# Softmax denominators as one row through HBM, with a different first and last chunk, in a conformer block

## The chip, the cores and the metric

The kernel runs on one core of one Trainium2 chip. The metric is the device time of one launch in microseconds (us). Five instruction streams matter: PE (TensorE, matrix multiply; its weight loads are listed as PEld), ACT (ScalarE, activation functions), DVE (VectorE, elementwise work and statistics), POOL (GpSimd) and SP (SyncE, which here only starts DMA transfers). SPq and ACTq are the streams of SP and ACT as issuers of DMA. The sixteen DMA engines move data between HBM and the on-chip memory; a DMA can also transpose a tile of 2-byte elements on its way.

## The reference

One conformer block on x of shape (2, 4000, 512) in bfloat16, with D = 512 and a feed-forward width F = 2048. LayerNorm has no weights.

```python
h = _layernorm(x);  x1 = x + 0.5 * (_silu(h @ w_ff1_a) @ w_ff1_b)
h = _layernorm(x1); q, k, v = h @ w_q, h @ w_k, h @ w_v
p = _softmax(einsum('btd,bsd->bts', q, k) * D ** -0.5)
x2 = x1 + einsum('bts,bsd->btd', p, v) @ w_o
a, b = split(_layernorm(x2) @ w_pw1);  h = a * _sigmoid(b)
dc = depthwise convolution of h over time with the 3 taps dw, then batch-normalized over all B*T rows
x3 = x2 + _silu(dc) @ w_pw2
h = _layernorm(x3); x4 = x3 + 0.5 * (_silu(h @ w_ff2_a) @ w_ff2_b)
return _layernorm(x4)
```

## The kernel before, in words

The 8,000 rows are cut into 16 chunks of 500 rows, each of four tiles of 125 rows (`TILE`). The running x stays on chip (`XT`), 125 partitions by 512 columns a tile. All matmuls but a few go through the helper `mm` (L458), so the profile gives them one line; the tile names tell them apart. `s` is one of four PSUM banks handed out in turn by `sbank`, `y` one of four accumulation banks.

The program runs in stages. `ff1` goes through the 16 chunks: LayerNorm, first matmul with `Wa` and Silu, second matmul with `Wb`, residual. Then `attention` goes through 16 groups of 500 queries, eight for each of the two batches. Then comes the convolution, then `ff2` through the 16 chunks, with the closing LayerNorm and the stores of the output.

The order of work is written out by hand. `lags` holds matmuls that are emitted some steps after the step that makes their operand. `after(n, fn)` has `fn` emitted n ticks later, and `tick` is called once at the end of each step. Within an engine, instructions run in the order in which they are emitted; `Sync` adds the semaphore waits that the buffers ask for. A DMA takes its semaphore from a small set used in rotation, and the queue that issues it also waits until the previous DMA on that semaphore has landed. A record (`Buf`) stands for a piece of memory; a write to it waits for the write and the reads before it.

An attention group has 32 steps kt, one for each tile of 125 keys (padded to 128). In each step PE makes the scores (four matmuls into an `s` bank), ACT their exponentials `P`, and DVE adds `P` to a running sum `acc` (L749; L746 in the first step). The matmuls of `P` with the values are emitted four steps later, into the four `y` banks. So a group's last values matmuls come in step 3 of the next group; `finish_queries` follows them. It copies the four `y` banks to `OT`, two on ACT (L483) and two on DVE (L787), and splits `acc` into a bfloat16 high part `ahi` (L791) and the rest `alo` (L792). Two ticks later `sums` turns these into the 500 denominators: for each of four tiles, two matmuls with the keys' partial sums as weights and a column of ones as the moving operand, which leaves the denominators on the query partitions of one PSUM tile, and a reciprocal on DVE (L802). From the fourth tick on, one a tick, `project` multiplies `OT` with the folded weights `Wvo` and the residual scales by the reciprocal (L591). When the last of the four is out, `done` starts the LayerNorm of the chunk (`ln_job`), whose last steps are four DMA transposes on SP (L491). Parts of the convolution (`conv_b`, `conv_a`, `taps_beside`) are emitted in steps 22 and 27 of the next group and 1 and 6 of the one after. In group 7 and the start of group 8 the keys of the second batch are loaded over those of the first (`second_keys`, one load and one DMA transpose on SP a step).

At the start (`program`) x's first chunk is loaded by two DMAs on SP, of 80 and 45 rows (`ROWS`), followed on SP by 16 weight loads with the second chunk of x among them. A Silu on one column brings ACT's table in, and 20 matmuls of zeros (`warm`) run on PE. The first chunk's normalized rows are transposed by PE (`transpose_pe`, L473) and copied out of PSUM by ACT and DVE. Further on, in the eighth step of the first chunk, `weights` has SP load w_q, w_k, w_v by DMA transposes and w_o by a plain DMA; `fold_weights` on PE needs them.

At the end `ff_last` handles the last chunk: it makes all 16 first matmuls, then all second matmuls tile by tile, so that the residual, LayerNorm and store of one tile run beside the matmuls of the next. Each tile's store is cut into 80 rows on SP and 45 on ACT (`store_out`, L665).

Of the kernel before, what the change touches and what calls it, by code (L numbers as in the profile page):

```python
# [52 lines left out]
class Sync:  # L53
# [105 lines left out]
    def dma(self, e, dkey, *fns, reads=(), writes=()):  # L159
        req = self._required(reads, writes)  # L160
        prev = self.count[dkey]
        if prev > 0:
            v = req.get(dkey)
            if v is None or v.val < prev:
                req[dkey] = Ev(dkey, prev, {})
        self._emit_waits(e, req)
        for fn in fns:
            fn(self.eng[e]).then_inc(self.sem[dkey], 16)
            self.count[dkey] += 16
        ev = Ev(dkey, self.count[dkey], dict(self.clock[e]))  # L170
        self._bind(ev, reads, writes)
        return ev
# [46 lines left out]
class Conformer:  # L219
    LN_SLOTS = 4  # L220
    NP = 8

    ROWS = ((0, 80), (80, TILE))
# [13 lines left out]
    def memory(self):  # L237
# [70 lines left out]
        self.zero, self.b_zero = self.P[0], self.b_P[0]  # L308
# [41 lines left out]

        self.late = [A.view(k * 1024, CHUNK) for k in range(FC - self.NP)]
        self.b_late = [A.buf("late", k * 1024, 1000) for k in range(FC - self.NP)]
# [44 lines left out]
        self.b_m3 = [C.buf("m3", oLT + 4096 + j * 250, 250) for j in range(TPC)]  # L397
        self.mx = small(TCB, parts=TILE)
# [9 lines left out]
        self.b_Y = [Buf("y%d" % i, excl=True) for i in range(4)]  # L408
        self.keys2 = nc.dram_tensor("keys2", [TB * 128, D], BF16, kind="Internal").ap()
# [51 lines left out]
    def warm(self, n):  # L461

        ps, b_ps = self.sbank()
        for k in range(n):
            self.mm(ps[:, 0:CHUNK], self.ident, self.zero, True, True, [self.b_ident, self.b_zero], b_ps,
                    inc=k == n - 1)

    def transpose_pe(self, ti, s, eng):

        ps, b_ps = self.sbank()  # L470
        out = ps[:, 0:DC * 64].bitcast(BF16).rearrange("p (c k) -> p c k", c=DC)
        for cc in range(DC):
            self.S.op("PE", lambda e, cc=cc: e.transpose(  # L473
                out[:, cc, 0:TILE], self.ltm[ti][0:TILE, cc * 128:(cc + 1) * 128], self.ident[0:TILE, 0:TILE]),
                reads=[self.b_ltm[ti], self.b_ident], writes=[b_ps], inc=cc == DC - 1)
        dst, src = self.lnT[s][:, ti, :, 0:TILE], out[:, :, 0:TILE]
        if eng == "ACT":
            self.act(dst, src, AF.Copy, [b_ps], [self.b_lnT[s][ti]])
        else:
            self.S.op("DVE", lambda e: e.tensor_copy(dst, src), reads=[b_ps], writes=[self.b_lnT[s][ti]])  # L480

# [3 lines left out]
    def load(self, dst, src, writes, eng="SP", reads=()):  # L485
        k = self.S.dsems[self.nxt("ld", 16)]
        return self.S.dma(eng, k, lambda e: e.dma_start(dst, src), reads=reads, writes=writes)  # L487

    def transpose(self, dst, src, reads, writes):
        k = self.S.dsems[16 + self.nxt("tr", 12)]  # L490
        return self.S.dma("SP", k, lambda e: e.dma_start_transpose(dst, src), reads=reads, writes=writes)  # L491

    def load_rows(self, dst, src, writes):
        k = self.S.dsems[self.nxt("ld", 16)]
        return self.S.dma("SP", k, *[lambda e, lo=lo, hi=hi: e.dma_start(dst[lo:hi], src[lo:hi])
                                     for lo, hi in self.ROWS], writes=writes)

# [4 lines left out]
    def load_x(self, c):  # L502
        if c == 0:
            src = self.x_flat[0:CHUNK, :].rearrange("(t p) d -> p t d", p=TILE)
            self.load_rows(self.XTc[0], src, self.bx[0:TPC])
# [90 lines left out]
    def ff_first(self, c, f, p, b_p):  # L596
        ps, b_ps = self.sbank()
        out = ps[:, 0:CHUNK].rearrange("p (t k) -> p t k", t=TPC)
        for cc in range(DC):
            self.mm(out, self.Wa[:, cc, f * 128:(f + 1) * 128], self.lnT[c % 2][:, :, cc, 0:TILE],  # L600
                    cc == 0, cc == DC - 1, [self.b_Wa[f * self.NWA // FC]] + self.b_lnT[c % 2], b_ps)
        self.act(p, ps[:, 0:CHUNK], AF.Silu, [b_ps], [b_p])

    def ff_second(self, f, ti, p, b_p, inc):
        self.mm(self.Yb[ti][0:TILE, :], p[:, ti * TILE:(ti + 1) * TILE], self.Wb[:, f, :],
                f == 0, f == FC - 1, [self.b_Wb[f], b_p], self.b_Y[ti], inc=inc)

    def ff_chunk(self, c, old, hook, done):

        pops = {0: old // 2, 1: old - old // 2, 2: 0, 3: 0, 7: 2, 11: 2}  # L610
        for f in range(FC):
            s = self.nxt("P", self.NP)
            self.ff_first(c, f, self.P[s], self.b_P[s])

            def second(f=f, s=s):
                for ti in range(TPC):
                    self.ff_second(f, ti, self.P[s], self.b_P[s], f == FC - 1 or ti == TPC - 1)
# [9 lines left out]

    def ff_last(self, c, old):

        S, late = self.S, FC - self.NP  # L630
        blocks = []
        for f in range(FC):
            if f < late:
                blocks.append((self.late[f], self.b_late[f]))
            else:
                s = self.nxt("P", self.NP)
                blocks.append((self.P[s], self.b_P[s]))
            self.ff_first(c, f, *blocks[f])
            self.pop({0: old // 2, 1: old - old // 2}.get(f, 0))
            self.tick()  # L640
        while self.later:
            self.tick()
        sl = self.nxt("ln", self.LN_SLOTS)
        for ti in range(TPC):
            for f in range(FC):
                self.ff_second(f, ti, *blocks[f], f == FC - 1)
            self.residual(self.Yb[ti][0:TILE, :], self.b_Y[ti], c * TPC + ti, 0.5)
            self.ln_stats(c, sl, ti)
            S.op("DVE", lambda e: e.bn_aggr(self.mv[sl][:, ti, :], self.st[sl][:, ti, :]),
                 reads=[self.b_st[sl][ti]], writes=[self.b_mv[sl][ti]])  # L650
            S.op("DVE", lambda e: e.tensor_scalar(self.va[sl][:, ti:ti + 1], self.mv[sl][:, ti, 1:2], EPS, None, ALU.add),
                 reads=[self.b_mv[sl][ti]], writes=[self.b_va[sl]])
            S.op("POOL", lambda e: e.tensor_tensor(out=self.rs[sl][:, ti:ti + 1], in0=self.va[sl][:, ti:ti + 1],
                                                   in1=self.neghalf[0:TILE, ti:ti + 1], op=ALU.pow),
                 reads=[self.b_va[sl], self.b_neghalf], writes=[self.b_rs[sl]])
            self.ln_norm(c, sl, ti, self.osb[0][:, ti, :], self.b_osb[0][ti], "DVE")
            self.store_out(c, self.osb[0], self.b_osb[0], ti, ti + 1, ("SP", "ACT"))

    def store_out(self, c, o, b_o, lo, hi, engs=("SP",)):
        dst = self.out_flat[c * CHUNK:(c + 1) * CHUNK, :].rearrange("(t p) d -> p t d", p=TILE)  # L660
        rows = self.ROWS if len(engs) > 1 else ((0, TILE),)
        for (r0, r1), eng in zip(rows, engs):
            k = self.S.dsems[28 + self.nxt("od", 8)]
# [558 lines left out]
```

## Time and profile before

| | |
|---|---|
| median of 3 runs | 2111.88 us (2107.25 to 2113.43) |
| profiled execution | 2107.25 us |
| its span, first to last instruction | 2103.5 us |
| PE busy | 2063.4 us, 9,708 matmuls |
| DVE busy | 1092.4 us |
| ACT busy | 733.8 us |
| mean granted PE clock | 0.995 |

All times inside the profile count from the start of the span. Busy time of PE is modelled from pipelined matmuls. A line of the waits says which engine and line waited for which, the total in us, how often, and the longest. A line of the timeline gives the start, the duration, engine, line, operation, written and read tiles, shapes, how many instructions are merged in the line, and in brackets how long the engine was idle before and what released it. A line of the windows gives for a stretch the busy time of PE, PEld, DVE, ACT and POOL with counts, then the granted clock, the mean busy share of the sixteen DMA engines and GB/s.

### The profile page before, as it was taken

What the parts mean: (1) busy time and instruction counts of PE and PEld (TensorE: products, weight loads), DVE (VectorE), ACT (ScalarE), POOL (GpSimd) and SP (SyncE); (2) the same over time, 40 slices, a digit from 0 to 9 for tenths busy, and PEclk for the clock granted to TensorE, in tenths of its full rate; (3) what the DMA queues carried; (4) which work ended last, traced back from release to release, by engine and by line L of the source; (5) the groups of instructions that cost most, each with busy time, mean ns of one, the idle gap of its engine ahead of it and who ended that gap; (6) DMA issues with size and microseconds to landing.
All of it is one profiled execution on the core that took longest, in us unless ns stands there. A gap on an engine that the chain in (4) does not pass through costs nothing.

```text
span 2103.5 us, 24444 instructions
## 1 busy us (share of the span) xinstructions
PE 2063.4 (98%) x9708; PEld 1040.7 (49%) x9710; DVE 1092.4 (52%) x2235; ACT 733.8 (35%) x1251; POOL 124.0 (6%) x260
## 2 busy tenths in 40 slices
PE   8999999999999999999999999999987999999998
PEld 4555555554444444444444444444443555555554
DVE  3345444324556566656665666566755344444433
ACT  3333333333333333333333333333325334434332
POOL 0111100000000000000000000000000000000000
PEclk9999999999999999999999999999999999999999
DMA  6222221110000000005300000000134011111111
GB/s 169 60 55 57 60 61 52 45 43 11 11 11 8 18 18 18 11 15 121 75 11 16 17 18 11 18 16 18 49 97 119 23 38 33 30 40 30 33 38 41
DMA packets 197262, 84.83 MB, mean 40 GB/s; under 512 B 145812, under 2 KB 196631, under 8 KB 197143
## 3 DMA queue, kind: packets, MB, share of 16 engines
q1 hardware_dynamic: 190567, 78.84, 15.2%
q10 hardware_dynamic: 6576, 4.38, 0.7%
q8 instruction: 78, 1.28, 0.3%
q14 instruction: 41, 0.34, 0.1%
HBM read 29.53 MB, written 19.04 MB: 23 GB/s over the span
## 4 chain that ended last, share of the span: by engine, by line
PE 94%; DVE 3%; SPq 1%; DMA 1%; ACT 1%; issue 0%; ACTq 0%; POOL 0%; POOLq 0%; DVEq 0%
PE s L458 54%; PE y L458 40%; DVE work L787 1%; SPq L491 1%; DVE work L792 1%; DMA xt<-in_x_dram 1%; DVE work L749 0%; ACT work L483 0%; DVE work L522 0%; DVE work L545 0%; DVE work L791 0%; ACTq L487 0%; SPq L487 0%; DMA keys<-in_w_o_dram 0%; POOL work L532 0%
## 5 line engine op out<-in xcount | busy, mean ns | idle before, releaser
L483 ACT ACTIVATE work<-s 128x500 bf16<-128x500 f32 (+2 forms) x1062 | 623.0, 587 | 1250.5 <-PE s L458 1240.4
L458 PE MATMUL s<-work,wff 128*128 128x500 bf16 x2560 | 629.8, 377 | 4.0 <-DVE wff L831 3.4
L458 PE MATMUL y<-work,keys 128*128 128x500 bf16 x2048 | 519.1, 374 | 1.2
L458 PE MATMUL s<-work,keys 128*128 128x500 bf16 x2048 | 517.4, 374 | 0.1
L458 PE MATMUL y<-wff,work 128*125 128x512 bf16 x2016 | 506.6, 379 | 0.0
L749 DVE TENSOR_TENSOR work<-work 128x500 f32<-128x500 f32 x496 | 334.7, 675 | 304.6 <-ACT work L483 302.8
L458 PEld LDWEIGHTS s<-work,wff 128*128 128x128 bf16 x2560 | 250.4, 98 | 284.1 <-DVE wff L831 3.9
L458 PEld LDWEIGHTS y<-wff,work 128*125 128x125 bf16 x2016 | 275.2, 137 | 173.5
L458 PEld LDWEIGHTS y<-work,keys 128*128 128x128 bf16 x2048 | 198.0, 97 | 244.3 <-DVE work L787 15.5
L458 PEld LDWEIGHTS s<-work,keys 128*128 128x128 bf16 x2048 | 199.2, 98 | 228.9 <-DVE work L678 0.6
L591 DVE SCALAR_TENSOR_TENSOR xt<-y,xt 125x512 bf16<-125x512 f32 x128 | 79.7, 682 | 369.2 <-PE y L458 369.2
L522 DVE BATCH_NORM_STATS2 work<-xt 125x6 f32<-125x512 bf16 x320 | 201.6, 679 | 9.4 <-DMA xt<-in_x_dram 9.3
L458 PE MATMUL s<-work 128*125 128x512 bf16 (+3 forms) x666 | 150.2, 349 | 22.2 <-DVE work L792 7.9
L532 POOL TENSOR_TENSOR work<-work 125x4 f32<-125x4 f32 x79 | 84.3, 1067 | 1147.9 <-DVE work L530 1147.9
L545 DVE TENSOR_SCALAR work<-xt,work 125x512 bf16<-125x512 bf16 x288 | 115.6, 447 | 21.5 <-POOL work L532 18.8
L458 PEld LDWEIGHTS s<-work 128*125 128x125 bf16 (+2 forms) x666 | 82.8, 137 | 76.5 <-issue 12.2
L591 DVE SCALAR_TENSOR_TENSOR xt<-s,xt 125x512 bf16<-125x512 f32 x64 | 43.7, 690 | 134.5 <-PE s L458 134.5
L831 DVE SCALAR_TENSOR_TENSOR wff<-wff,s 128x500 bf16<-128x500 f32 x64 | 43.2, 677 | 63.1 <-PE s L458 63.1
L483 ACT ACTIVATE wff<-s 128x500 f32<-128x500 f32 x64 | 37.6, 587 | 79.7 <-PE s L458 75.2
L591 DVE SCALAR_TENSOR_TENSOR xt<-s,work,xt 125x512 bf16<-125x512 f32 x64 | 48.1, 751 | 33.1 <-PE s L458 32.2
L458 PE MATMUL s<-keys,work 128*128 128x500 bf16 x256 | 64.4, 376 | 0.0
L483 ACT ACTIVATE work<-keys,work 128x500 bf16<-128x500 bf16 x64 | 49.6, 794 | 5.9 <-DMA wff<-in_w_ff_a_dram 3.7
(61 smaller groups left out, 420.8 us busy)
## 6 DMA issues: line engine op xcount, KB each, us to landing
xt<-in_x_dram SPq DMA_DIRECT2D x15, 500.0 KB
out_dram<-work SPq DMA_DIRECT2D x15, 500.0 KB
dcvd<-wff SPq DMA_DIRECT2D x52, 125.0 KB, 1.7
keys<-dcvd SPq DMA_DIRECT2D x13, 500.0 KB, 5.1
keys<-work SPq DMA_DIRECT2D x8, 512.0 KB, 3.6
keys<-keys SPq DMA_DIRECT2D x32, 128.0 KB, 2.3
work<-work SPq DMA_TRANSPOSE x188, 2.5
wff<-in_w_ff_a_dram SPq DMA_DIRECT2D x8, 256.0 KB, 5.3
```

Source lines behind the costliest of these rows:

```text
L458: self.S.op("PE", lambda e: e.matmul(out, lhsT, rhs, start=start, stop=stop), reads=reads, writes=[bank], inc=stop if inc is None else inc)
L483: return self.S.op("ACT", lambda e: e.activation(out, in_, func, **kw), reads=reads, writes=writes)
L491: return self.S.dma("SP", k, lambda e: e.dma_start_transpose(dst, src), reads=reads, writes=writes)
L522: self.S.op("DVE", lambda e: e.bn_stats(self.st[sl][:, ti, :], self.XT[g]), reads=[self.bx[g]], writes=[self.b_st[sl][ti]])
L532: S.op("POOL", lambda e: e.tensor_tensor(out=self.rs[sl], in0=self.va[sl], in1=self.neghalf[0:TILE, :], op=ALU.pow), reads=[self.b_va[sl], ...
L545: self.S.op("DVE", lambda e: e.tensor_scalar(out, self.XT[g], self.mv[sl][:, ti, 0:1], self.rs[sl][:, ti:ti + 1], ALU.subtract, ALU.mult), ...
L591: self.S.op("DVE", lambda e: e.scalar_tensor_tensor(out=self.XT[g], in0=ps, scalar=scalar, in1=self.XT[g], op0=ALU.mult, op1=ALU.add), rea ...
L749: S.op("DVE", lambda e, p=p: e.tensor_tensor(out=self.acc[s], in0=self.acc[s], in1=self.P[p], op=ALU.add), reads=[self.b_P[p], self.b_acc[ ...
L787: S.op("DVE", lambda e, dc=dc: e.tensor_copy(self.OT[:, dc, :], self.Yb[dc][:, 0:CHUNK]), reads=[self.b_Y[dc]], writes=[self.b_OT[dc]])
L792: S.op("DVE", lambda e: e.tensor_tensor(out=self.alo, in0=self.acc[s], in1=self.ahi, op=ALU.subtract), reads=[self.b_acc[s], self.b_ahi], ...
L831: self.S.op("DVE", lambda e: e.scalar_tensor_tensor(out=self.G[gs][:, jj, 1:1 + CHUNK], in0=self.th[k], scalar=1.0, in1=ps[:, 0:CHUNK], op ...
```

## The change

There are three parts.

In attention, `split_sums` emits L791 and L792 right after the last addition of a group, in step 31. `finish_queries` calls `sum_row` at once for all groups but the last: two matmuls with the ones column as weights and `ahi`, then `alo`, as moving operands give the 500 denominators as one row on one partition; ACT copies the row, SP stores it to HBM (`rowd`), and SP loads it back onto the query partitions, 125 by 4. The reciprocal is emitted five ticks on, the projections from the sixth tick instead of the fourth. The last group keeps `sums`.

At the start, x's first chunk is loaded as four tiles of 125 rows on SP, the weights are loaded from ACT's queue, and the second chunk of x is loaded after them, on SP. The Silu on one column, `warm` and `transpose_pe` go; the first chunk is transposed by DMA on SP. Loads have 12 semaphores instead of 16, transposes 16 instead of 12.

At the end `ff_last` goes; the last chunk is handled as the others are, with its closing LayerNorm emitted without gaps and one store per tile of 125 rows on SP. The stores of a chunk share one record, `b_out`.

```diff
     def load(self, dst, src, writes, eng="SP", reads=()):
-        k = self.S.dsems[self.nxt("ld", 16)]
+        k = self.S.dsems[self.nxt("ld", 12)]
...
     def transpose(self, dst, src, reads, writes):
-        k = self.S.dsems[16 + self.nxt("tr", 12)]
+        k = self.S.dsems[12 + self.nxt("tr", 16)]
...
     def load_x(self, c):
         if c == 0:
-            src = self.x_flat[0:CHUNK, :].rearrange("(t p) d -> p t d", p=TILE)
-            self.load_rows(self.XTc[0], src, self.bx[0:TPC])
+            for ti in range(TPC):
+                self.load(self.XT[ti], self.x_flat[ti * TILE:(ti + 1) * TILE, :], [self.bx[ti]])
...
+                if kt == TB - 1:
+                    self.split_sums(s)
+
                 def values(kt=kt, p=p, b=b, qc=qc):
...
+    def split_sums(self, s):
+
+        S = self.S
+        S.op("DVE", lambda e: e.tensor_copy(self.ahi, self.acc[s]), reads=[self.b_acc[s]], writes=[self.b_ahi])
+        S.op("DVE", lambda e: e.tensor_tensor(out=self.alo, in0=self.acc[s], in1=self.ahi, op=ALU.subtract),
+             reads=[self.b_acc[s], self.b_ahi], writes=[self.b_alo])
+
     def finish_queries(self, b, qc, done):
...
-        S.op("DVE", lambda e: e.tensor_copy(self.ahi, self.acc[s]), reads=[self.b_acc[s]], writes=[self.b_ahi])
-        S.op("DVE", lambda e: e.tensor_tensor(out=self.alo, in0=self.acc[s], in1=self.ahi, op=ALU.subtract),
-             reads=[self.b_acc[s], self.b_ahi], writes=[self.b_alo])
+
+        def sum_row():
+            ps, b_ps = self.sbank()
+            for part, bp in ((self.ahi, self.b_ahi), (self.alo, self.b_alo)):
+                self.mm(ps[0:1, 0:CHUNK], self.onec[:, 0:1], part, part is self.ahi, part is self.alo,
+                        [bp, self.b_onec], b_ps)
+            self.act(self.row, ps[0:1, 0:CHUNK], AF.Copy, [b_ps], [self.b_row])
+            self.store(self.rowd[s:s + 1, :], self.row, [self.b_row], [self.b_rowd[s]])
+            k = S.dsems[self.nxt("ld", 12)]
+            S.dma("SP", k, lambda e: e.dma_start(self.sq[s], self.rowd[s].rearrange("(t p) -> p t", p=TILE),
+                                                 allow_slow_non_contiguous=True),
+                  reads=[self.b_rowd[s]], writes=[self.b_sq[s]])
...
         last = b * TCB + qc == NCK - 1
-        self.after(1 if last else 2, sums)
+        if last:
+            self.after(1, sums)
+        else:
+            sum_row()
+            self.after(5, lambda: S.op("DVE", lambda e: e.reciprocal(self.rl[s], self.sq[s]),
+                                       reads=[self.b_sq[s]], writes=[self.b_rl[s]]))
         for ti in range(TPC):
-            self.after((2 if last else 4) + ti, lambda ti=ti: project(ti))
+            self.after((2 if last else 6) + ti, lambda ti=ti: project(ti))
...
-    def out_job(self, c, at):
+    def out_job(self, c, at, gap=1):
...
+            lo = ti if last else 0
+            if last or ti == TPC - 1:
+                k = self.S.dsems[28 + self.nxt("od", 8)]
+                ev = self.S.dma("SP", k, lambda e: e.dma_start(dst[:, lo:ti + 1, :], self.osb[o][:, lo:ti + 1, :]),
+                                reads=self.b_osb[o][lo:ti + 1], writes=[self.b_out[c]])
...
         self.load_x(0)
         for k in range(self.NWA):
-            self.load_wa(i["w_ff1_a"], k)
-            self.load_wb(i["w_ff1_b"], 2 * k, 2 * k + 2)
-            if k == 3:
-                self.load_x(1)
+            self.load_wa(i["w_ff1_a"], k, "ACT")
+            self.load_wb(i["w_ff1_b"], 2 * k, 2 * k + 2, "ACT")
+        self.load_x(1)
...
-        self.act(self.nr1, self.onef, AF.Silu, [self.b_onef], [self.b_nr1])
-
-        self.warm(20)
...
-        for ti in range(TPC):
-            self.transpose_pe(ti, 0, ("ACT", "DVE")[ti % 2])
+            self.transpose(self.lnT[0][:, ti], self.ltm[ti], [self.b_ltm[ti]], [self.b_lnT[0][ti]])
...
-            self.ff_chunk(c, old, hook, lambda: self.out_job(c, 5))
-
-        for c in range(NCK - 1):
+            self.ff_chunk(c, old, hook, lambda: self.out_job(c, 5 if c < NCK - 1 else 0, 1 if c < NCK - 1 else 0))
+
+        for c in range(NCK):
             ff2(c, len(self.lags) if c else 0)
-        self.ff_last(NCK - 1, len(self.lags))
```

## The prediction

> **What bounds the kernel now.** I read the page first: busy time, then the chain that ended last.
>
> ```profile
> PE 2063.4 (98%) x9708; PEld 1040.7 (49%) x9710; DVE 1092.4 (52%) x2235; ACT 733.8 (35%) x1251; POOL 124.0 (6%) x260
> ...
> PE 94%; DVE 3%; SPq 1%; DMA 1%; ACT 1%; issue 0%; ACTq 0%; POOL 0%; POOLq 0%; DVEq 0%
> ```
>
> TensorE (PE) is the bound. Time moves only where the change opens or closes a gap in PE: at the sixteen attention group ends, at the start, or at the end. Next, the waits (total us, times, longest); L787, L791 and L792 all run once or twice per group end.
>
> ```profile
> PEld y L458 <- DVE work L787: 15.5, 30, 0.6
> PEld s L458 <- DVE work L792: 9.3, 16, 0.6
> PEld s L458 <- DVE work L791: 5.5, 16, 2.0
> ```
>
> The timeline of the first group end (start, us, engine, line):
>
> ```profile
> 526.89 0.59 ACT L483 ACTIVATE work<-s 128x500 bf16<-128x500 f32 x1 [1.10 <-PE s L458]
> 527.47 1.01 PE L458 MATMUL s<-work,keys 128*128 128x500 bf16 x4
> 528.10 1.25 DVE L787 CAST work<-y 128x500 bf16<-128x500 f32 x2
> 528.58 0.59 ACT L483 ACTIVATE work<-s 128x500 bf16<-128x500 f32 x1
> 529.41 0.10 PEld L458 LDWEIGHTS y<-work,keys 128*128 128x128 bf16 x1 [0.47 <-DVE work L787]
> 529.72 0.68 DVE L792 TENSOR_TENSOR work<-work 128x500 bf16<-128x500 f32 x1
> 530.45 0.56 PE L458 MATMUL s<-work 128*125 128x1 bf16 x7 [0.50 <-DVE work L792]
> 530.88 1.01 PE L458 MATMUL s<-work,keys 128*128 128x500 bf16 x4
> 531.99 0.59 ACT L483 ACTIVATE work<-s 128x500 bf16<-128x500 f32 x1 [2.82 <-PE s L458]
> ```
>
> Exponentials normally come every 1.69 us (526.89 to 528.58); across the sums they are 3.41 apart. So a group end loses 1.72 us: a wait for the second L787 cast, then the one-column matmuls, which wait for L791 and L792 behind the casts in VectorE's (DVE's) order.
>
> Then start and end, timeline and windows (PE, PEld, DVE, ACT, POOL, clock, DMA share, GB/s):
>
> ```profile
> 10.00 1.38 DVE L545 TENSOR_SCALAR work<-xt,work 125x512 bf16<-125x512 bf16 x4 [1.15 <-POOL work L532]
> 12.44 5.76 PE L458 MATMUL s<-work,wff 128*128 128x500 bf16 x20 [0.61 <-DVE work L480]
> 24.06 5.25 SPq L491 DMA_TRANSPOSE work<-work  x4
> 41.67 1.02 PE L458 MATMUL s<-keys 128*128 128x512 bf16 x4 [1.72 <-DMA keys<-in_w_o_dram]
> ...
> 2098.12 0.69 DVE L591 SCALAR_TENSOR_TENSOR xt<-y,xt 125x512 bf16<-125x512 f32 x1 [0.56 <-PE y L458]
> 2100.60 0.41 DVE L545 TENSOR_SCALAR work<-xt,work 125x512 bf16<-125x512 bf16 x1 [0.66 <-POOL work L653]
> ```
> ```profile
> 22.00:23.00 1.00, 1.00 (x7) 0.46 (x6) 0.95 (x1) 0.25 (x1) 1.00 (x4) 1.00 0.34 118
> 2081.50:2082.00 0.50, 0.50 (x5) 0.22 (x3) 0.00 (x0) 0.25 (x1) 0.00 (x0) 1.00 0.32 106
> 2102.00:2102.50 0.50, 0.00 (x0) 0.00 (x0) 0.00 (x0) 0.00 (x0) 0.00 (x0) 0.50 0.85 228
> ```
>
> The first two windows hold 125-row transfers (x's third chunk; an output chunk). Their share, 0.32 to 0.34 of sixteen engines, is five engines at full work, 106 to 118 GB/s. The last window holds the closing store, split into 80 and 45 rows: 0.85.
>
> **Group ends.** L791 and L792 move ahead, into the slot after the previous group's last addition, where DVE idles about 1.0 us an iteration. Two row matmuls of 500 columns (0.21 us each, the spacing of 500-column matmuls) come directly after the last values matmuls, so scores begin at 527.90 instead of 527.47 and the next values at 528.74. These still wait for the second cast, loading weights at 529.41; that wait hides the 0.43. Their last matmul ends near 529.72 and scores follow, against 530.88: 1.16 saved. Fifteen times: -17.4. Without that cover the two matmuls cost 0.43 x 15 = 6.5.
>
> The last group keeps its eight matmuls, but their operands are ready early: PE's idle 1.50 and 0.50 us there (waits for L791 and L792 at 1558.61 and 1559.33) go; the second cast, done at 1558.22, is before the projection needs it. -2.0. ScalarE's (ACT's) row copy (0.59 by its other 500-column copies) fits between its two casts' end, 528.43, and the next exponential, then 529.0. Together -19.4.
>
> **The round trip.** Counted from the exponential's end at 527.48, the row is copied at +1.5. Store: 1.7 to landing, as the dcvd stores; the gather is issued at +3.35, its data starts 0.85 later (output store: issued 2079.70, data from 2080.5) and needs 0.35 for the receipt (1.7 less 0.85 and 0.5 of data). No row shows 4-byte pieces. The transposes of 899 to 906 move 2,176 packets in 2.6 us of all sixteen engines, 19 ns each; 1 KB store packets take 4.75 us x 5 / 500 = 47 ns. With 100 pieces on each of five engines: 1.9 to 4.7 us; all on one engine: 9.5 to 23.5. I take five, as all other 125-row transfers. Arrival +6.5 to +9.3. The reciprocal, five ticks on, comes to DVE at +8 without convolution work and +9.7 with it. Behind it on DVE stand additions, taps and residuals. PE feels it only when the third projection needs the first one's bank, about +13.5. The Trainium skill's page "DMA: Bandwidth & Descriptors", section "Rules for kernel authors", speaks against this gather: a strided last dimension makes one descriptor per element. By that rule the count is the 500 assumed here and the sum stays; no row shows it.
>
> SP waits for the row, then for its store, some 2 us. Queued behind are convolution stores and, once, three of the second batch's key loads, needed 25 iterations later. Projections and the LayerNorm after them come two iterations later: the last transposes leave at iteration 17, for use at 22, five iterations or 10 us against 6. In group 7 SP's key loads leave little of that; I allow 0.5 us.
>
> **Start.** PE starts at 12.44. Now x's four 125-row tiles run on SP's queue beside weights on ACT's. Chunk 1's load is ahead of the transposes on SP; with twelve load semaphores in rotation it first waits for the fifth weight load. At 118 GB/s the four tiles (500 KB) take 4.3 us alone, from 1.7 to 6.0; sharing five engines evenly with weights, 8.6, so they land at 10.7. The last statistics (0.62) and the 1.64 from statistics to the first normalize (8.36 to 10.00) give 13.0; first transpose at 13.4. Chunk 1's 500 KB stand before its data: 8.6 more, to 19.3. Four transposes: 2.6 us of all engines, 5.2 if shared, then receipt: 24.9; I take 24.5.
>
> Bounds: with nothing shared, transposes leave at 9.1, four issues of 1.3 follow, the last lands 2.5 after its issue, 15.5. With everything shared at the start's slower rate (chunk 1 landed at 17.96 after 260 KB on each of its engines in 16 us, 16 KB/us), x takes 12.2, chunk 1 another 12.2, transposes 5.2: 32. The skill's section "Queues, rings and completion order" on that page has the engines alternate between queues by packet. By it the shared value holds; without it the sum would be up to 9 less. No row has both queues loaded.
>
> The shift 24.5 - 12.44 = 12.1 is partly given back: PE's 2.9 us of waiting for w_k (1.2) and w_o (1.7) vanish, as SP's chain starts at 24 to 30 instead of 24.06 and PE arrives 12 later. Dropping the warming matmuls: the granted clock was 0.50 from 12 to 15 in spite of them; 0.2. The first Silu's table load, 1.28, falls while PE fills four free banks (over 3.4 us): nothing; 1.3 without that cover. Start: +9.4, bounds +0.4 and +16.9.
>
> **End.** PE's last matmul ends at 2098.10, the span 5.4 later. Now four residuals (2.4 net of overlap) and the chain statistics, aggregate, power, first normalize (4.54, as 2074.16 to 2078.70) put the first store at +6.4. Each 125-row store writes the same buffer record, so SP waits for each to land: 0.85, data 1.19 (a quarter of 4.75), 0.35, a wait of 0.08: 2.47, four times 9.9; then 0.7 to the end as before. 17.0 less 5.4: +11.6. With data at 0.5, +8.8; with receipts 0.4 slower, +13.2.
>
> **Sum.** -19.4 + 0.5 + 9.4 + 11.6 = +2.1 on the profiled execution's 2107.25 (span 2103.5 and 3.75 around it): 2109.4. The median shown, 2111.88, is 4.6 above it: 2114.0.
>
> **Rivals.** *Cheap start* (transposes not behind x and weights): +0.4 there, total -6.9: 2105. For it: weights are issued in bursts, and one queue may run dry. Against: both begin in the first us, and the five engines carry 100 KB of x and 100 KB of chunk 1 each. 0.15, two thirds of it faster by over 0.3%.
>
> *Slower, congested start* (16 KB/us, 32 us): total +9.6: 2121.5. For it: the rate the start shows. Against: eleven engines run out early and leave bandwidth. It decides from a first matmul at 29. 0.2.
>
> *Slower, gather late*: beyond about 9 us of gather PE waits at every group end, 15 us per us; at 23.5 us some 210 in all. Against: the price per packet must double, or one engine take all. 0.06.
>
> *Row not hidden* (the change gives less than it says): the two matmuls add to PE, +6.5: 2120.5. For it: nothing, unless ACT's copies free their banks later. 0.07.
>
> **How the numbers follow.** Forecast case 0.52: 2114, own range 2108 to 2119. About 0.3%, 6.3 us, is what a measurement of this kernel tells from no change. Faster 0.10 from the cheap start; slower 0.2 + 0.06 + 0.07 and 0.03 of the forecast's upper edge, 0.36; within 0.54. Range 2105 to 2123 leaves out the late gather and the edges.
>
> **What would show it.** L787's waits near 0.1 us per group end, none for L791 or L792, exponentials at most 2.2 apart there; reciprocal idle under 2 us; first feed-forward matmul near 24.5, no wait for w_o; four closing stores 2.5 apart, the end 17 after the last matmul. A first matmul below 18, or exponentials still over 3 apart, makes it wrong.

## The result, and the profile after

| | before | after |
|---|---|---|
| median, runs beside each other | 2109.57 us (2107.03 to 2113.43) | 2118.46 us (2117.57 to 2120.55) |
| ratio, 95% interval | | 1.0042 (1.0022 to 1.0062) |
| span of the profiled execution | 2103.5 us | 2113.7 us |
| PE's last matmul ends | 2098.08 | 2096.45 |

The change costs 8.9 us (by the interval 4.6 to 13.1). The page of after, busy time and the chain that ended last:

```profile
PE 2050.4 (97%) x9582; PEld 1032.4 (49%) x9584; DVE 1090.0 (52%) x2229; ACT 739.3 (35%) x1263; POOL 118.7 (6%) x257
...
PE 95%; issue 1%; DVE 1%; DMA 1%; SPq 0%; POOL 0%; ACT 0%; POOLq 0%; ACTq 0%; DVEq 0%
```

PE does less work and is still the bound; 97% instead of 98% says that it stands idle for longer. The timeline of after at the first group end, the place shown for before:

```profile
541.30 0.59 ACT L464 ACTIVATE work<-s 128x500 bf16<-128x500 f32 x1 [1.10 <-PE s L460]
541.98 0.58 PE L460 MATMUL s<-work 128*1 128x500 bf16 x2
542.49 1.02 PE L460 MATMUL s<-work,keys 128*128 128x500 bf16 x4
542.51 1.25 DVE L728 CAST work<-y 128x500 bf16<-128x500 f32 x2
542.72 0.56 ACT L464 ACTIVATE work<-s 1x500 f32<-1x500 f32 x1
543.35 1.00 PE L460 MATMUL y<-work,keys 128*128 128x500 bf16 x4
543.55 0.59 ACT L464 ACTIVATE work<-s 128x500 bf16<-128x500 f32 x1 [0.27 <-PE s L460]
544.19 1.01 PE L460 MATMUL s<-work,keys 128*128 128x500 bf16 x4
545.24 0.59 ACT L464 ACTIVATE work<-s 128x500 bf16<-128x500 f32 x1 [1.10 <-PE s L460]
```

PE runs through: the four values matmuls take 1.00 us in one piece, though the casts (now L728) still run beside them, and the exponentials are 2.25 apart instead of 3.41. The wait of weight loads for those casts (in the list of waits: total, times, longest) is down from 15.5 us to this, and the lines of the split are gone from the list:

```profile
PEld y L460 <- DVE work L728: 0.2, 1, 0.2
```

The start of after, timeline, then the waits of SP's queue:

```profile
13.99 1.38 DVE L521 TENSOR_SCALAR work<-xt,work 125x512 bf16<-125x512 bf16 x4 [1.15 <-POOL work L508]
14.43 10.22 SPq L472 DMA_TRANSPOSE work<-work  x4
28.85 6.80 PE L460 MATMUL s<-work,wff 128*128 128x500 bf16 x20 [28.85 <-DMA work<-work]
```
```profile
SPq L468 <- DMA wff<-in_w_ff_a_dram: 10.4, 1, 10.4
```

The first feed-forward matmul is at 28.85 (12.44 before). The transposes go out from 14.43, but take 10.22 us to issue and 14.4 to land. Ahead of them on SP the load of x's second chunk (chunk 1; the chunks count from 0) stood 10.4 us for a weight load's semaphore. The end of after: timeline, windows (columns as in the prediction), and SP's waits from 2100 on:

```profile
2093.70 2.75 PE L460 MATMUL y<-wff,work 128*125 128x512 bf16 x12
2095.84 2.48 DVE L567 SCALAR_TENSOR_TENSOR xt<-y,xt 125x512 bf16<-125x512 f32 x4 [17.79 <-PE y L460]
2102.39 1.38 DVE L521 TENSOR_SCALAR work<-xt,work 125x512 bf16<-125x512 bf16 x4 [1.20 <-POOL work L508]
2102.82 8.47 SPq L912 DMA_DIRECT2D out_dram<-work  x4
```
```profile
2107.00:2108.00 1.00, 0.00 (x0) 0.00 (x0) 0.00 (x0) 0.00 (x0) 0.00 (x0) 0.50 0.30 94
2108.00:2109.00 1.00, 0.00 (x0) 0.00 (x0) 0.00 (x0) 0.00 (x0) 0.00 (x0) 0.50 0.04 11
2109.00:2110.00 1.00, 0.00 (x0) 0.00 (x0) 0.00 (x0) 0.00 (x0) 0.00 (x0) 0.50 0.25 69
```
```profile
SPq L912 <- DMA out_dram<-work: 7.2, 3, 2.7
```

The four stores are issued over 8.47 us, and between their data the engines stand nearly still (0.04): each waits for the one before. The span ends 17.2 us after PE's last matmul.

How far after lags behind before, read at the same instruction in both traces: +14.4 at the first copy of `acc` (466.51 to 480.92), -3.6 when the last group's end is past, -1.63 at the end of PE's last matmul, +10.2 at the end of the span.

### The profile page after: what moved, and what is told of

Read it like the earlier page. It is cut to its first block, busy times and chain, and to the rows that moved or that the text cites. A ratio compares the mean times of both kernels' runs of the same rounds, so it can differ in the third digit from the quotient of the medians.

```text
span 2113.7 us, 24196 instructions
## 1 busy us (share of the span) xinstructions
PE 2050.4 (97%) x9582; PEld 1032.4 (49%) x9584; DVE 1090.0 (52%) x2229; ACT 739.3 (35%) x1263; POOL 118.7 (6%) x257
## 4 chain that ended last, share of the span: by engine, by line
PE 95%; issue 1%; DVE 1%; DMA 1%; SPq 0%; POOL 0%; ACT 0%; POOLq 0%; ACTq 0%; DVEq 0%
PE s L460 54%; PE y L460 41%; DMA xt<-in_x_dram 0%; DVE work L498 0%; SPq L472 0%; DMA work<-work 0%; DVE work L521 0%; POOL work L508 0%; DVE xt L567 0%; DMA wff<-in_w_ff_b_dram 0%; DMA wff<-in_w_ff_a_dram 0%; DVE wff L851 0%; DVE wff L786 0%; DVE work L504 0%; SPq L468 0%
## 5 line engine op out<-in xcount | busy, mean ns | idle before, releaser
L464 ACT ACTIVATE work<-s 128x500 bf16<-128x500 f32 (+1 forms) x1083 | 635.3, 587 | 1244.0 <-PE s L460 1242.7
L460 PE MATMUL y<-wff,work 128*125 128x512 bf16 x2048 | 514.8, 379 | 0.0
L460 PEld LDWEIGHTS y<-wff,work 128*125 128x125 bf16 x2048 | 279.6, 137 | 176.4
L460 PE MATMUL s<-work 128*125 128x512 bf16 (+2 forms) x556 | 140.7, 377 | 12.2 <-ACT work L464 8.8
L460 PEld LDWEIGHTS s<-work 128*125 128x125 bf16 (+1 forms) x556 | 72.5, 134 | 64.1 <-ACT work L464 11.5
```

Source lines behind the costliest of these rows:

```text
L460: self.S.op("PE", lambda e: e.matmul(out, lhsT, rhs, start=start, stop=stop), reads=reads, writes=[bank], inc=stop if inc is None else inc)
L464: return self.S.op("ACT", lambda e: e.activation(out, in_, func, **kw), reads=reads, writes=writes)
```

## Experiments: the three parts alone

Each part was put by itself on the kernel before.

```diff
 rows_only: split_sums, sum_row and the later ticks as in the change; start and end of before
 start_only: loads, queues, semaphores and DMA transposes as in the change; the rest of before
 end_only: no ff_last; out_job with four stores on one record; the rest of before
```

> The attention part of the change alone, on the kernel before, with its start, its end and its 16 load semaphores. Theory (three separate terms): each group end gives back about 1.04 us, the last one about 2.8, so PE reaches the convolution some 18 us earlier; of that, 1 to 2 us may be lost again before the second feed-forward stage, where the same stretch was 1.9 longer in the changed kernel. About 16 to 18 us less than before, 2092 to 2094. Rival (the parts hang together: the attention part gains only because a late start had moved it): under 10 us. First feed-forward matmul stays at 12.4.

> The start of the change alone: four x tiles on SP, weights from ACT, second chunk after them, DMA transposes, no warming matmuls, 12 load semaphores. Theory: PE's first feed-forward matmul at about 28.9 instead of 12.4, of which 2.9 is given back where PE no longer waits for w_k and w_o, and 1.0 is lost to a cold clock: 14.4 us more than before, about 2124. Rival (the prediction's price): 9.4 more. Second rival (the delay is absorbed later in the first stage): under 5 more.

> The end of the change alone. Theory: 11.8 us more than before (17.2 from PE's last matmul to the end of the span instead of 5.4), about 2121.5. Rival (part of it is an effect of the other parts, as the last chunk's PE work is ordered differently): the time from PE's last matmul stays 17 but PE ends 1 us or more later or earlier than in the kernel before.

| kernel | median, us | ratio to before (95%) | against before's 2107.99 |
|---|---|---|---|
| rows_only | 2091.10 | 0.9917 (0.9903 to 0.9931) | -16.9 |
| start_only | 2122.20 | 1.0069 (1.0055 to 1.0083) | +14.2 |
| end_only | 2119.37 | 1.0059 (1.0045 to 1.0073) | +11.4 |

The sum is +8.7; the whole change is +8.9. Each interval is some 3 us wide to either side, and within that the parts add up; no effect of one on another shows. So each can be judged alone: a gain in attention, given back and more by the start and the end.

## Experiments: what gains at a group end

Two kernels part the order on DVE from the row. Both emit the split (L791 and L792) in step 31 as the change does, and send nothing through HBM.

```diff
 split_only
+                if kt == TB - 1:
+                    self.split_sums(s)
 cols_early, this as well, with the projections at their old ticks:
-        self.after(1 if last else 2, sums)
+        if last:
+            self.after(1, sums)
+        else:
+            sums()
```

> The kernel before with only this moved: the split of the sums into two parts is emitted after a group's last addition, and the eight one-column matmuls follow the last values matmuls at once, with no row, no HBM and the projections at their old place. Theory (the gain is the order, not the row: work put where PE waits for VectorE's casts is free): as much as the row, 1.0 to 1.1 us a group end and 2.8 at the last, 16 to 18 us less than before, 2092 to 2094. Rival (the row's two long matmuls are the gain): the eight small matmuls take 0.56 against the row's 0.51, so no more than 0.1 per group end separates them if both are covered; if the weight loads of 125 columns are not covered, up to 0.5 less per group end, 8 us less gain.

> The kernel before with one thing alone: L791 and L792 are emitted in step 31 of a group, as in the change; the eight one-column matmuls, the reciprocal and the projections stay at their old ticks, and nothing goes through HBM. Theory (what is gained at a group end is DVE's order: the split no longer stands behind the two casts): the waits for L791 and L792 go, 14.8 us in the whole profile of before (0.93 a group); the wait for the second cast, 0.47 at the first group end, stays, since the sums still come after the next scores. So about 68.4 to 68.6 a group instead of 69.42, and 13 to 16 us less than before in all. Rival (the row form is what saves, two matmuls in place of eight): at most a third of that, under 6 us. Time by the theory 2094 (2091 to 2097), by the rival above 2102.

cols_early took 2088.90 us, ratio 0.9911 (0.9896 to 0.9927), 19.1 us less than before where 16 to 18 were expected; split_only 2093.79, ratio 0.9918 (0.9901 to 0.9935), as its theory had it and far from its rival. The intervals of the three attention variants overlap; the trace tells them apart. Per group, from one copy of `acc` to that of the next, mean of the last 13: before 69.42 us, split_only 68.63, the row 68.40, cols_early 68.22. Split_only at the first group end, timeline (the casts are L797 in these two kernels):

```profile
527.82 0.11 PEld L458 LDWEIGHTS y<-work,keys 128*128 128x128 bf16 x2 [0.62 <-DVE work L797]
528.40 0.10 PEld L458 LDWEIGHTS y<-work,keys 128*128 128x128 bf16 x1 [0.47 <-DVE work L797]
528.63 0.57 PE L458 MATMUL s<-work 128*125 128x1 bf16 x8
```

The eight matmuls run in one piece, 0.57 us, without a wait for the split; the wait for the casts (0.47) is still there. So moving two DVE instructions gives 0.79 of the 1.02 us a group. The rest comes from putting the sums between the last values matmuls and the next scores, where they fill time in which the casts work: moving them there is all that parts cols_early from split_only. In the timeline of cols_early:

```profile
526.57 0.57 PE L458 MATMUL s<-work 128*125 128x1 bf16 x8
527.00 1.01 PE L458 MATMUL s<-work,keys 128*128 128x500 bf16 x4
527.20 1.26 DVE L797 CAST work<-y 128x500 bf16<-128x500 f32 x2
```

Eight one-column matmuls in the same place do it as well as two of 500 columns and are some 0.2 us a group ahead of them. The row, its copy, its trip through HBM and the later projections gain nothing by themselves.

> The changed kernel with the reciprocal emitted two ticks after the last values matmuls instead of five, so that DVE waits for the gathered denominators and the end of its wait shows when they land. Prediction's estimate: row copied at 1.5 after the last exponential before it, denominators 5.0 to 7.8 after that (4-byte pieces 19 to 47 ns each on five engines): reciprocal starts 5.0 to 8 us after the row copy ends. Rival (all pieces on one engine): over 13. The DVE wait itself should not reach PE, within 1 us of the changed kernel's span, as additions have several iterations of slack.

```diff
-            self.after(5, lambda: S.op("DVE", lambda e: e.reciprocal(self.rl[s], self.sq[s]),
+            self.after(2, lambda: S.op("DVE", lambda e: e.reciprocal(self.rl[s], self.sq[s]),
```

With the reciprocal asked for early, DVE has to wait for the gathered row, and its start shows when the row is there. (One run, 2118.05 us: within the changed kernel's runs.) Timeline, then the DMA queue's packets from 544.5 to 546.6:

```profile
542.70 0.56 ACT L464 ACTIVATE work<-s 1x500 f32<-1x500 f32 x1
543.28 0.26 SPq L476 DMA_DIRECT2D rowd<-work  x1
544.50 0.29 SPq L741 DMA_DIRECT2D work<-rowd  x1
546.54 0.18 DVE L770 RECIPROCAL work<-work 125x4 f32<-125x4 f32 x1 [1.71 <-DMA work<-rowd]
```
```profile
q1 hardware_dynamic: 505, 0.00, 13.3%
```

The round trip takes 3.3 us from the copied row, not the 5.0 to 8 of the estimate; the gather is 2.0 of it. The reciprocals are first needed by the residual at 552.00: over 5 us to spare, so the late gather was no danger. 13.3% of sixteen engines over 2.1 us, 4.5 us of engine time, makes 9 ns a packet, where the prediction had 19 to 47. From 545.40 to 546.25 the busy share is 0.33, the work of five engines, as it assumed.

The Trainium skill's page "DMA: Bandwidth & Descriptors", section "Rules for kernel authors", has one descriptor per element for a strided last dimension; the 505 packets, one for each of 500 elements and five more, agree with that.

## Experiments: the start

Five kernels. The first three edit the changed kernel; start_pe and no_warm edit the kernel before.

```diff
 start_x1_behind: self.load_x(1) after the four transposes instead of before them
 start_x_split: each x tile loaded as 80 and 45 rows
 start_sems16: 16 load semaphores in rotation, 12 for transposes
 start_pe: the change's loads and queues, but transpose_pe, copies on DVE; no warm(20), no early Silu
 no_warm: before without self.warm(20)
```

> The changed kernel with one line moved: the load of x's second chunk is issued on SP after the first chunk's four transposes instead of before them. In the changed kernel that load was issued at 12.5, landed at 24.5, and the transposes behind it let PE start at 28.85. Theory (the transposes stand behind the second chunk's 500 KB on five engines): x's first chunk still lands at 11.7 and the transposes leave from 14.4, but land at 20 to 21, so PE starts at 20.5 to 21.5; the second chunk lands at about 25 and is not missed; 6 to 8 us less than the changed kernel, about 2111. Rival (the weights on ACT's queue hold the transposes up, not the second chunk): PE starts at 26 or later, less than 3 us saved.

> The changed kernel with each of x's four first tiles loaded by two DMAs, of 80 and 45 rows, on one semaphore. Theory: 125-row DMAs use five engines and split ones almost all, so the fourth tile lands at 7 to 8 instead of 11.7 and the first normalize comes 4 us earlier, at about 10; but the second chunk's load, still of 125 rows, still stands before the transposes, so PE starts only 1 to 3 us earlier than 28.85. Rival (x's landing sets PE's start): 4 us earlier, below 25. Second rival (the split does not matter while weights share the engines): the fourth tile lands after 10.5.

> The changed kernel with sixteen load semaphores in rotation again (and twelve for transposes) instead of twelve and sixteen; nothing else. Chunk 1's load is the 21st load, so its semaphore is then that of the first weight load (behind x's four tiles) instead of the fifth, and SP no longer stands 10.4 us for it. Theory (the prediction's arithmetic held but for this wait: it took the load as issued in time to run straight on behind x's tiles): chunk 1's load is issued by 6, x's tiles land unchanged to 0.5 us, chunk 1 lands at 19 to 21 instead of 24.5, the four transposes are issued in 5 to 6 us instead of 10.2, first feed-forward matmul at 23.5 to 25 instead of 28.85, total 3 to 5 us under the changed kernel: 2113.5 to 2115.5. Rival (the five engines' shared rate alone sets chunk 1's end, whenever it is issued): chunk 1 still lands after 23, first matmul after 27.5, total within 1.5 us of the changed kernel. Third reading: the earlier load takes x's last tiles' time, the first normalize moves from 13.99 to 16 or later, and the gain is under 2.

> The start of the changed kernel on the kernel before, but the first chunk is still transposed by PE (all four copies on DVE, since ACT is issuing weight loads): four 125-row tiles of x on SP, weights from ACT's queue, chunk 1 behind them, no warming matmuls, no early Silu. Theory (of the start's loss the loads of x cost some 4 us and the transposes by DMA behind chunk 1's load the rest): first normalize at 14.0 as in the changed kernel, 2.4 from there to the first matmul as before, so 16.4 to 17.5; PE then waits a little for w_k and w_o again; total 3 to 6 us over before. Rival (the late x tiles and the shared queues set the start, and PE transposes only move the wait to the weights): first matmul still later than 22 or waits of several us for wff behind it, total over 9 us above before.

> The kernel before without the 20 matmuls of zeros at its start; all else stays. The prediction put them at 0.2 us, from one execution in which the clock was 0.50 from 12 to 15 in spite of them. Theory now (in other executions of the same start they keep the clock: 4.41 us for the first 20 matmuls instead of 5.76): without them the first 20 matmuls take 5.8 to 7.0 and the first attention landmark moves by 1.3 to 2.5 us. By the prediction's reading: within 0.3 of before. Read from the trace; the total can't show it.

| kernel | last x tile's statistics start | chunk 1's statistics start | transposes issued over | first matmul | median, us (ratio to before) |
|---|---|---|---|---|---|
| after | 11.66 | 24.50 | 10.22 | 28.85 | 2118.46 (1.0042) |
| start_x_split, one run | 11.30 | 21.27 | 7.47 | 26.75 | 2115.55 |
| start_sems16 | 11.60 | 18.92 | 5.28 | 27.80 | 2116.11 (1.0034, 1.0022 to 1.0046) |
| start_x1_behind | 11.65 | 27.95 | 5.33 | 24.00 | 2113.88 (1.0022, 1.0012 to 1.0031) |
| start_pe | 11.69 | 24.84 | none | 16.97 | 2119.32 (1.0039, 1.0027 to 1.0052) |

Each ratio is to the runs of before made beside that kernel, whose medians lie between 2108.12 and 2109.72. So differences of a us or two between these totals mean little; the times in the table say more.

**Chunk 1's load costs 4.9 us at the first matmul.** With the load behind the transposes the first matmul comes at 24.00, between the theory (20.5 to 21.5) and its rival (26 or later). The first copy of `acc` comes 4.5 us earlier than in after (476.38 against 480.92). The total falls by 4.6 by the medians, by 3.5 if each kernel is set against the before beside it; the theory had 6 to 8. The transposes are not free even so: 9.6 us pass from the first issue to the first matmul.

**The semaphore alone does not decide it.** With sixteen semaphores the wait of SP's queue (list of waits) is down from 10.4 us to

```profile
SPq L468 <- DMA wff<-in_w_ff_a_dram: 3.0, 1, 3.0
```

and chunk 1 lands at 18.92, as the theory had it. Yet the first matmul comes at 27.80 and not by 25. ACT's last weight load is now issued by 21.5 instead of 16.6, and the weights share the engines with the transposes. The DMA queues of start_sems16 from 22 to 24 (q10 holds ACT's loads, q1 SP's; the last figure is the time of the packets as a share of sixteen engines, and the two add up to more than 100%):

```profile
q10 hardware_dynamic: 434, 0.27, 92.0%
q1 hardware_dynamic: 510, 0.12, 35.3%
```

What moves before the last transpose lands is the same as in the changed kernel (x, the weights, chunk 1, the transposes), and it is over only 1.05 us sooner. Theory and rival were half right: the landing of the first, the first matmul of the second. The total, 2.3 us under after's median and 0.9 by the differences to before, decides nothing. That the weights hold the transposes up fits these rows; no run took the weights away.

**Cutting the x tiles brings them 0.4 us earlier.** So the landing went as the second rival had it, and the first matmul, 2.1 us earlier, as the theory had it: SP's wait for the semaphore is 6.1 us here instead of 10.4, and chunk 1 comes 3.2 us sooner. In the window from 4 to 8 of after the sixteen engines are all at work, which may be why the cut gave so little:

```profile
4.00:8.00 4.00, 0.00 (x0) 0.00 (x0) 1.39 (x2) 0.00 (x0) 0.00 (x0) 1.00 1.01 288
```

**PE's transposes hand the wait on.** start_pe has its first matmul at 16.97, as expected, but its total is 9.6 over before, not 3 to 6. Chunk 1's late arrival delays SP's whole chain, its own transposes (issued at 30.95; 24.06 in before) and those of w_q and w_k behind them, and PE meets that later (timeline and window of start_pe):

```profile
44.03 1.48 PE L458 MATMUL s<-keys 128*128 128x512 bf16 x3 [3.82 <-DMA keys<-in_w_k_dram]
```
```profile
44.00:48.00 4.00, 3.97 (x10) 1.73 (x10) 0.00 (x0) 1.87 (x4) 0.00 (x0) 0.50 0.79 219
```

Behind the idle 3.82 us the granted clock is 0.50, so the wait is paid a second time. The rival was right that a weight wait follows; it is w_k that is late, not wff. What the slower matmuls cost there was not measured apart.

**The warming matmuls stay open.** no_warm (one run, 2110.30 us) needs 5.97 us for the first 20 matmuls. With them the profiles show 5.76 (before) and 5.77 (split_only), but also 4.41 (rows_only, end_only, cols_early). So they are worth 0.2 or 1.6 us by execution. The first copy of `acc`, 466.73, comes 0.2 after before's and 1.1 to 1.8 after that of the other four. The prediction's 0.2 was read from one execution.

## Experiment: the end

```diff
-                                reads=self.b_osb[o][lo:ti + 1], writes=[self.b_out[c]])
+                                reads=self.b_osb[o][lo:ti + 1], writes=[Buf("out")])
```

> The changed kernel with a record of its own for each output store, so that the four closing stores no longer wait for each other. Theory (17.2 from PE's last matmul to the end are 6.4 to the first store, four serial stores of 2.5 and 0.8): the stores are issued about 0.35 apart, behind the normalizations, and run on the same five engines; last store issued at 7.6 after PE's end, data of four tiles 4.8 in a row from about 7.3, so the end comes at 13 instead of 17.2, 4 us saved, about 2114. Rival (the engines, not the waits, set it; the four stores share five engines anyway): under 2 saved. Second rival (each store is short, the wait is all): 6.5 or more saved.

2113.79 us, ratio 1.0021 (1.0012 to 1.0031): 4.7 us under the changed kernel. Timeline and windows of it:

```profile
2103.39 1.64 SPq L912 DMA_DIRECT2D out_dram<-work  x4
```
```profile
2105.00:2106.00 1.00, 0.00 (x0) 0.00 (x0) 0.00 (x0) 0.00 (x0) 0.00 (x0) 0.50 0.35 107
2106.00:2107.00 1.00, 0.00 (x0) 0.00 (x0) 0.00 (x0) 0.00 (x0) 0.00 (x0) 0.50 0.32 101
2107.00:2108.00 1.00, 0.00 (x0) 0.00 (x0) 0.00 (x0) 0.00 (x0) 0.00 (x0) 0.50 0.36 125
2108.00:2109.00 1.00, 0.00 (x0) 0.00 (x0) 0.00 (x0) 0.00 (x0) 0.00 (x0) 0.50 0.30 104
```

The four stores go out within 1.64 us and their data run without a gap, at the rate of five engines. The span ends 13.6 us after PE's last matmul (2097.02) instead of 17.2: the shared record costs 3.6, near the theory's 4 (the totals say 4.7 by the medians and 3.6 by the differences to before). The other 8.2 over before's 5.4 are the chain of the last chunk, which stands behind all of its matmuls, and 125-row stores; these two were not measured apart.

## Why the prediction was right or wrong

The forecast was 2114.0 and the time is 2118.46: inside the range, but the predicted difference was +2.1 and the measured one is +8.9. That the two times lie only 4.5 us apart is in part luck: the forecast adds its difference to the median it was shown, 2111.88, and before's median in the runs beside after is 2109.57.

| term | predicted | in the two profiles | part alone |
|---|---|---|---|
| group ends, with group 7 and the last | -18.9 | -18.0 | -16.9 |
| start | +9.4 | +14.4 | +14.2 |
| stage change after attention | none | +2.0 | |
| end | +11.6 | +11.8 | +11.4 |
| sum | +2.1 | +10.2 | +8.7 |

**Group ends: right in mechanism, the sizes off and partly cancelling.** The wait for the second cast hid the two row matmuls, as argued: left alone it is still 0.47 in split_only, and by the prediction's 0.43 the exponentials would be some 2.7 apart without that cover, not 2.25. At the first group end the long step gives the 1.16 that was forecast (3.41 to 2.25). But the step behind it was 0.06 shorter than normal in before and no longer is; and from the second group end on, three steps in a row take 1.75 + 3.35 + 1.63 = 6.73 us before and 2.31 + 1.69 + 1.69 = 5.69 after. That leaves 1.04, and 1.02 a group on average, where 1.16 was taken for all fifteen. The last group's end gives 2.8 instead of 2.0, and group 7, for which 0.5 was allowed, takes the 68.38 us of the others; these two bring the sum back to -18.0. The mechanism is that of the order on DVE and of the place of the sums; the row form, which the prediction credited with the gain, is not needed for it.

**Start: the step that failed.** It is the path from x's tiles to the first matmul, priced at 24.5 and measured at 28.85. The x tiles came about as worked out: the last statistics at 11.66 (predicted 10.7), first normalize at 13.99 (13.0). Then chunk 1 was to land at 19.3 and came at 24.50, for the wait on its semaphore was named but not priced: the load was taken as running straight on behind x. The four transposes were to need 5.2 us after chunk 1. In after they take 4.4, but that is no confirmation, since the first of them had been issued at 14.43, long before: in start_sems16, where chunk 1 does come at 18.92, they need 8.9, and in start_x1_behind, with no chunk 1 ahead of them, 9.6 from the first issue (the prediction's lower bound has 6.4 for that with nothing shared). So an early chunk 1 alone would not have brought the forecast's 24.5. The weights that ACT still loads were left out of that step. The waits for w_k and w_o vanished as said; these two lines of before's waits (2.9 us together) have no counterpart in after:

```profile
PE s L458 <- DMA keys<-in_w_o_dram: 1.7, 1, 1.7
PE s L458 <- DMA keys<-in_w_k_dram: 1.2, 1, 1.2
```

Slower first matmuls make up the rest: the first 20 took 6.80 us against 5.76, 1.0 where the prediction had 0.2.

**The congested start** named a first matmul from 29 on as its mark and +9.6 as its total; 28.85 just misses the one and +8.9 is close to the other. It was the better forecast, though its rate was not what happened: x's tiles landed some 2 us sooner than it had them. The forecast case priced the queue's contents one after the other, the transposes as if little else moved; that was its error.

**Queues.** A row with both queues loaded now exists. DMA queues of after, 2 to 8:

```profile
q10 hardware_dynamic: 1768, 1.11, 66.1%
q1 hardware_dynamic: 355, 0.35, 19.6%
```

19.6% of sixteen engines is 3.1, of the five that the prediction counts for a 125-row tile. So by the time of its packets SP gets more than half of them.

That fits the Trainium skill's statement that engines alternate between queues by packet ("DMA: Bandwidth & Descriptors", "Queues, rings and completion order"); the alternation itself is not shown.

**End: right.** First store 6.4 after the last matmul as predicted, though the prediction's two terms, 2.4 and 4.54, add up to 6.9; the trace has 1.8 and 4.6. Then the stores are 2.74 apart on average (2.47) and the last issue is 2.7 before the end (3.2): two small errors that cancel in the 17.2 (17.0). The shared record does what was said of it.

**The cheap start, the late gather and the row not hidden fell**: first matmul far above 15.5; gather 2.0 us; exponentials 2.25 apart. **The stage change** was foreseen by nothing, and no effect of the change shows in it: from the last copy of `acc` to the first closing matmul of the convolution the seven profiled kernels with the row need 103.1 to 105.3 us, and the one shown is the slowest of them; the five with before's attention spread as far, 106.7 to 108.7, and before, at 106.9, is near their fast end.

## What to carry to other kernels

When an instruction waits behind others on its engine, first try to emit it earlier: two lines moved on DVE gave most of the gain here, and cols_early, with the shortest groups of all and 2088.90 us, has no new data path at all. Price a queue by all that must move before the needed piece lands, on every queue that shares the engines, and price each semaphore that its issuer stands for. A store per tile with one shared record is a chain of round trips (3.6 us here); give each its own.

## What the runs showed that was not expected

The clock of PE at the change of stage differs from execution to execution after the same idle time. The second group of 32 closing matmuls of the convolution, before, then rows_only, then cols_early (timeline):

```profile
1610.93 7.09 PE L458 MATMUL s<-work 128*125 128x512 bf16 x32 [3.39 <-DVE xt L591]
```
```profile
1592.11 9.91 PE L465 MATMUL s<-work 128*125 128x512 bf16 x32 [3.39 <-DVE xt L598]
```
```profile
1588.82 8.78 PE L458 MATMUL s<-work 128*125 128x512 bf16 x32 [3.39 <-DVE xt L591]
```

PE has been idle for 3.39 us in each. In the windows that hold the start of them the granted clock is 1.00 in before and 0.60 in rows_only:

```profile
1610.00:1615.00 5.00, 4.07 (x19) 2.65 (x20) 4.83 (x9) 0.53 (x1) 0.00 (x0) 1.00 0.54 105
```
```profile
1590.00:1595.00 5.00, 2.89 (x7) 1.67 (x8) 4.45 (x9) 1.70 (x3) 0.00 (x0) 0.60 0.40 80
```

Of 14 profiled kernels six show 7.09, three 8.78 and five 9.84 to 9.97, whatever was changed in them.

The Trainium skill's page "TensorE: Matmul & The Clock Gate", section "Part 1: The HAM clock gate", describes an activity window of about 3.4 us that runs freely; an idle stretch just as long would then be seen or missed by where it falls. The numbers agree with that, but no run here shows the window itself. Up to 2.9 us of a difference between two single profiles of this kernel can come from the clock at this one place.
